# SBUF pool order, first loads and output store of a bandwidth-bound decode kernel

## The chip, the cores and the metric

One core of one Trainium2 chip runs the whole kernel. The metric is the device time of one execution in microseconds (us), as the median of several executions. The profile's span (first to last instruction) is about 1.8 us shorter than that time. A kernel's executions agree to about 0.15% either way, so differences of a few tenths of a per cent need several rounds.

Three sources are used. The *profile* is one traced execution, with its page and its views (chain of waits, windows, timeline). The *packet records* of the same trace hold start, duration and size of each DMA packet (one contiguous piece that one of the 16 DMA engines moves), but not which engine it was. The *built program* holds each tile's address in SBUF, the on-chip memory of 128 partitions into which the loads go. In the views PE is TensorE, PEld its weight loads, DVE VectorE, ACT ScalarE and POOL GpSimd; SyncE (SP) only issues loads and stores and waits.

## The reference

A decode step: `xn = layernorm(x)`, then `x + attention(xn) + mlp(xn)`, for 4 batch rows of width 576.

```python
# attention: 32 query heads, 16 K/V heads, a window of the last 2048 of 8192 positions, head size 128
q = (xn @ wq) ;  k, v = k_cache[:, :, Sk - W:], v_cache[:, :, Sk - W:]
o = softmax(q k^T * 128**-0.5) v ;  attn = o @ wo
# mlp (w1 and w2 drop out: with one position every shifted group is zero)
h2 = gelu(layernorm(xn) @ w3) @ w4
out = x + attn + xn + h2
```

The kernel must read 64 MB of K and V (1024 x 1024 bytes to the MB here; 16 heads, 2 MB each of K and V) and 19 MB of weights: 87.17 million bytes in all. It computes very little per byte.

## The kernel before

Everything is loaded in one sequence on the SyncE queue: x, wq, then K and V head by head, w3 after the third V, wo in four parts, w4 at the end. Seven K/V buffers let the loads run ahead. Pools are laid out in SBUF in the order in which they are opened.

```python
const = ctx.enter_context(tc.tile_pool(name="const", bufs=1))      # small tiles of many sizes
small = ctx.enter_context(tc.tile_pool(name="small", bufs=2))
kvp   = ctx.enter_context(tc.tile_pool(name="kv", bufs=NKV))       # NKV = 7, 16 KB per partition each
ktp, ptp = ...                                                     # work tiles (cut)
wp    = ctx.enter_context(tc.tile_pool(name="w", bufs=1))          # wq, later w3, later w4
wop   = ctx.enter_context(tc.tile_pool(name="wo", bufs=2))
...
x_bf = const.tile([B, D], BF16)
nc.sync.dma_start(out=x_bf[:], in_=x2)
wq_main = A_wq[0:KJ * P, :].rearrange("(p j) n -> p j n", j=KJ)
for j in range(KJ):                                                # 4 loads, 8 KB per partition
    nc.sync.dma_start(out=wq_sb[:, j * NQ:(j + 1) * NQ], in_=wq_main[:, j, :])
...
def load_kv(kind, h):                                              # one DMA, 128 packets of 16 KB
    t = kvp.tile([P, NC, Dh], BF16, tag="kv", name=f"{kind.lower()}n")
    nc.sync.dma_start(out=t[:].rearrange("p c d -> p (c d)"),
                      in_=win[:, h].rearrange("b (p c) d -> p b (c d)", c=NC))
...
W4_PIECES = [0, NFH // 2, NFH, NFH + 9, NFH + 14, NF]              # w4 in five loads, the last small
...
def acc_matmuls(lhsT, rhs):          # output: 4 column groups, batch rows at partitions 0,32,64,96 + b
    for i in range(NQD):
        nc.tensor.matmul(out=acc[i * QD:i * QD + B, :], lhsT=lhsT, rhs=rhs[:, i * CW:(i + 1) * CW], ...)
...
nc.vector.tensor_copy(out=fin[:], in_=acc[:])
for i in range(NQD):                                               # four output stores, two queues
    eng = nc.sync if i % 2 == 0 else nc.scalar
    eng.dma_start(out=o2[:, i * CW:(i + 1) * CW], in_=fin[i * QD:i * QD + B, :])
```

## Time and profile before

| | before |
|---|---|
| time, median | 216.3 us (216.18 to 216.32, 3 runs) |
| HBM read | 87.17 MB, 428 GB/s in the middle of the run |
| first wq packet starts | 2.15 us |
| last w4 load lands | 210.21 us |
| start of the final cast to the end of the span | 3.61 us |

These are lines of the page of the kernel before: the span, each engine's busy share, then for 40 equal slices the busy share of the DMA engines in tenths and the rate, and at the end the queue that fetches instructions (packets, MB, share).

```profile
span 214.6 us, 6449 instructions
## 1 busy us (share of the span) xinstructions
PE 121.0 (56%) x2893; PEld 94.9 (44%) x2893; DVE 118.0 (55%) x223; ACT 70.1 (33%) x258; POOL 6.1 (3%) x14
...
DMA  5999999999999999999999999999999999999960
GB/s 207 429 437 434 428 429 425 425 425 437 426 429 423 437 431 419 439 425 434 431 428 425 428 428 430 422 434 431 429 418 428 437 419 425 437 427 422 419 262 12
DMA packets 7123, 87.58 MB, mean 408 GB/s; under 512 B 820, under 2 KB 824, under 8 KB 1336
...
q8 instruction: 22, 0.36, 0.6%
...
```

No compute engine is near full, and the DMA row is at 9 from the second slice to the third last. This kernel is as long as its load stream plus the two ends of it. The windows view of the same kernel shows how much of each stretch the DMA engines used; the last two columns are their busy share and the rate in GB/s.

```profile
core 0: us, PE busy (x) PEld busy (x) DVE busy (x) ACT busy (x) POOL busy (x), PEclk, DMA share, GB/s
0.00:2.00 2.00, 0.00 (x0) 0.00 (x0) 0.64 (x2) 0.00 (x0) 1.31 (x10) 1.00 0.01 2
2.00:14.00 12.00, 3.99 (x122) 3.76 (x123) 5.78 (x10) 0.00 (x0) 4.29 (x3) 1.00 1.00 403
14.00:200.00 186.00, 109.72 (x2551) 85.51 (x2548) 109.87 (x205) 68.29 (x252) 0.54 (x1) 1.00 1.01 428
200.00:205.00 5.00, 4.12 (x123) 3.36 (x124) 1.35 (x5) 1.83 (x7) 0.00 (x0) 1.00 1.00 417
205.00:208.00 3.00, 1.71 (x81) 1.36 (x74) 0.09 (x1) 0.00 (x0) 0.00 (x0) 1.00 0.59 244
208.00:212.00 4.00, 1.42 (x36) 0.89 (x35) 0.31 (x1) 0.00 (x0) 0.00 (x0) 0.59 0.15 58
...
```

The stream holds 428 GB/s for 186 us. It has not begun in the first two microseconds, and from 205 us on it dies away: some DMA engines have finished and others have not. The end of the chain of waits (start, length, what) says what the end waits for: the last load, the last 16 matmuls, the cast.

```profile
...
182.78 27.43 DMA w_sb<-in_B_w_dram
210.21 0.04 issue
210.26 0.68 PE acc L247 x16
210.93 0.02 issue
210.96 0.31 DVE fin L480
```

On the SyncE timeline the first issue is x, so wq's first issue starts only at 1.16 us; the last line holds two of the four stores. The other two stand on the ACT timeline, shown after it.

```profile
0.73 0.36 SPq L87 DMA_DIRECT2D x_bf<-in_A_x_dram  x1
1.16 2.06 SPq L92 DMA_DIRECT2D wq_sb<-in_A_wq_dram  x4
3.26 0.44 SPq L93 DMA_DIRECT2D wq_sb<-in_A_wq_dram  x1
...
211.29 0.63 SPq L483 DMA_DIRECT2D out_dram<-fin  x2
```

```profile
211.30 0.92 ACTq L483 DMA_DIRECT2D out_dram<-fin  x2
```

### The profile page before, as it was taken

The page shows a single profiled execution, that of the slowest core. Times are in us where ns is not written, and L with a number is a line of the kernel's source. Part 1 is how long each engine was busy: PE and PEld are TensorE (multiplying, and loading weights), DVE is VectorE, ACT ScalarE, POOL GpSimd, SP SyncE. Part 2 cuts the span into 40 slices and gives each one's busy share as a digit, 9 for nine tenths or more (in the row PEclk, how much of TensorE's full clock was granted, in tenths as well). Part 3 has the DMA queues.
Part 4 walks back from the last instruction along what each step waited for, and adds up shares of the span by engine and source line. Part 5 has one row for each costly group of instructions (what it writes and reads, how often), then busy time and mean ns, then how long its engine had stood idle before and what let it go on. Part 6 is the DMA issues. An engine that isn't in the chain of part 4 may idle for free. (4 is left out here: it accounts for less than half of the span.)

```text
span 214.6 us, 6449 instructions
## 1 busy us (share of the span) xinstructions
PE 121.0 (56%) x2893; PEld 94.9 (44%) x2893; DVE 118.0 (55%) x223; ACT 70.1 (33%) x258; POOL 6.1 (3%) x14
## 2 busy tenths in 40 slices
PE   0461355647470017157999577677474705779752
PEld 0350143445360015145899456555453604557641
DVE  5608799766470047348610798785573924854210
ACT  0000005571634001607070045570725340709600
POOL 5400100000000000000000000000000000000000
PEclk9999999999999999999999999999999999999995
DMA  5999999999999999999999999999999999999960
GB/s 207 429 437 434 428 429 425 425 425 437 426 429 423 437 431 419 439 425 434 431 428 425 428 428 430 422 434 431 429 418 428 437 419 425 437 427 422 419 262 12
DMA packets 7123, 87.58 MB, mean 408 GB/s; under 512 B 820, under 2 KB 824, under 8 KB 1336
## 3 DMA queue, kind: packets, MB, share of 16 engines
q1 hardware_dynamic: 7080, 87.17, 95.7%
q8 instruction: 22, 0.36, 0.6%
q14 instruction: 5, 0.04, 0.0%
q10 hardware_dynamic: 16, 0.00, 0.0%
HBM read 87.17 MB, written 0.00 MB: 406 GB/s over the span
## 5 line engine op out<-in xcount | busy, mean ns | idle before, releaser
L302 ACT ACTIVATE pt<-S 32x128 bf16<-32x128 f32 x256 | 68.5, 268 | 92.0 <-issue 55.3
L259 DVE STREAM_TRANSPOSE kt<-kn 128x1024 int32<-128x1024 int32 x64 | 74.3, 1205 | 11.4 <-DMA kn<-in_A_k_cache_dram 11.4
L313 PE MATMUL O<-pt,vn 128*128 128x8 bf16 x1024 | 37.4, 169 | 43.2 <-DMA vn<-in_A_v_cache_dram 41.7
L313 PEld LDWEIGHTS <-vn 128*128 128x128 bf16 x1024 | 34.4, 105 | 51.3 <-DMA vn<-in_A_v_cache_dram 43.6
L273 PE MATMUL S<-qz,kt 128*128 128x32 bf16 x1024 | 39.1, 189 | 25.2 <-DVE kt L259 25.2
L273 PEld LDWEIGHTS <-kt 128*128 128x128 bf16 x1024 | 33.6, 106 | 36.1 <-DVE kt L259 30.4
L287 DVE TENSOR_REDUCE m<-mxT 8x1 f32<-8x128 f32 x16 | 4.4, 277 | 42.6 <-PE mxT L285 42.6
L316 PE MATMUL O<-pt,ones_bf 128*128 128x64 bf16 x128 | 17.1, 226 | 0.0
L302 ACT ACT_TABLE_LOAD x1 | 1.3, 1283 | 32.6 <-DVE mx L280 32.6
L368 PEld LDWEIGHTS <-w_sb 128*128 128x128 bf16 x144 | 11.4, 164 | 0.5 <-issue 0.4
L368 PE MATMUL AB<-ln2T,w_sb 128*128 128x4 bf16 x144 | 11.5, 202 | 0.0
L280 DVE TENSOR_REDUCE mx<-S 128x8 f32<-128x512 f32 x16 | 10.4, 652 | 1.0 <-PE S L273 1.0
L295 PE MATMUL S<-dg,ones_bf 8*128 8x512 bf16 x16 | 9.6, 601 | 0.1
L265 PE MATMUL S<-negbig,ohT 4*128 4x512 bf16 x16 | 9.6, 601 | 0.0
L316 PEld LDWEIGHTS <-ones_bf 128*128 128x128 bf16 x128 | 8.4, 104 | 0.0
L370 PE MATMUL AB<-ln2T,w_sb 128*128 128x4 bf16 x36 | 7.3, 202 | 0.0
L247 PE MATMUL acc<-w_sb,gT 128*4 128x144 bf16 x144 | 4.8, 294 | 2.8 <-DMA w_sb<-in_B_w_dram 2.8
L324 DVE TENSOR_REDUCE dn<-O 128x8 f32<-128x64 f32 x16 | 3.3, 208 | 5.5 <-PE O L316 5.5
L375 DVE COPY g_x<-AB 128x144 f32<-128x144 f32 x1 | 0.3, 307 | 10.7 <-PE AB L370 10.7
L285 PE MATMUL mxT<-ident_f,mx 128*8 128x128 f32 x16 | 6.0, 374 | 0.3 <-DVE mx L280 0.3
L370 PEld LDWEIGHTS <-w_sb 128*128 128x128 bf16 x36 | 5.9, 165 | 0.0
L247 PEld LDWEIGHTS <-gT 128*4 128x4 bf16 x144 | 3.4, 104 | 3.6 <-issue 3.5
(72 smaller groups left out, 64.9 us busy)
## 6 DMA issues: line engine op xcount, KB each, us to landing
kn<-in_A_k_cache_dram SPq DMA_DIRECT2D x16, 2048.0 KB, 29.3
vn<-in_A_v_cache_dram SPq DMA_DIRECT2D x16, 2048.0 KB, 27.0
wo_sb<-in_A_wo_dram SPq DMA_DIRECT2D x4, 1152.0 KB, 28.8
w_sb<-in_B_w_dram SPq DMA_DIRECT2D x2, 2304.0 KB, 31.8
wq_sb<-in_A_wq_dram SPq DMA_DIRECT2D x4, 1024.0 KB, 4.9
w_sb<-in_B_w_dram SPq DMA_DIRECT2D x3, 1296.0 KB, 32.8
w_sb<-in_B_w_dram SPq DMA_DIRECT2D x2, 576.0 KB, 32.2
w_sb<-in_B_w_dram SPq DMA_DIRECT2D x1, 720.0 KB
```

Of the source, the lines that this page charges most:

```text
L247: nc.tensor.matmul(out=acc[i * QD:i * QD + B, :], lhsT=lhsT, rhs=rhs[:, i * CW:(i + 1) * CW], start=False, stop=False, skip_group_check=True)
L259: nc.vector.transpose(out=kt[:], in_=src)
L265: nc.tensor.matmul(out=S_ps[h][:].rearrange("p g k j -> p (g k) j"), lhsT=ohT[:], rhs=nb, start=True, stop=False, skip_group_check=True)
L273: nc.tensor.matmul(out=S_ps[h][:, s * (SC // NQD) + g].rearrange("p k j -> p (k j)"), lhsT=kt[:, ib, g * NQD:(g + 1) * NQD, e:2 * QD:2].re ...
L280: nc.vector.reduce_max(out=mx[:], in_=S_ps[h][:].rearrange("p g k j -> p j (g k)"), axis=AX.X)
L285: nc.tensor.transpose(out=mxT[:], in_=st[h][:], identity=ident_f[:])
L295: nc.tensor.matmul(out=S_ps[h][:].rearrange("p g k j -> p (g k) j"), lhsT=ones_bf[0:NJ, :], rhs=dg, start=False, stop=False, skip_group_ch ...
L302: nc.scalar.activation(out=PT[h][kb * QD:(kb + 1) * QD, :, c4, :], in_=S_ps[h][c4 * QD:(c4 + 1) * QD, :, kb, :], func=ACT.Exp, scale=scale)
L313: nc.tensor.matmul(out=O_ps[h][:, 0:NJ], lhsT=vn[:, g * NQD + s, :], rhs=pt[:, g, s, :], start=(g == 0 and s == 0), stop=False, skip_group ...
L316: nc.tensor.matmul(out=O_ps[h][:, NJ:].rearrange("p (c j) -> p c j", j=NJ), lhsT=ones_bf[:], rhs=pt[:, g:g + DG, s, :], start=False, stop= ...
L368: nc.tensor.matmul(out=g_ps[:, i, :], lhsT=w3[:, j * F + e * (F // 2) + f0:j * F + (e + 1) * (F // 2):NFH], rhs=ln2T[:, j, :], start=False ...
L370: nc.tensor.matmul(out=g_ps[:, i, :], lhsT=w3[:, KJ * F + f0:KJ * F + F // 2:NFH], rhs=ln2T[:, KJ + e, :], start=False, stop=False, skip_g ...
```

## The change

Its intent, as far as the code tells it: start the weight stream earlier and with larger packets, keep the big tiles' addresses independent of the small ones, and end with one store instead of four. For the one store the batch rows must stand at equal distances, so each group of 32 partitions holds its 4 rows 8 apart, and the left operand of the accumulation gets 32 columns, of which 28 are zero.

```diff
+    kvp = ctx.enter_context(tc.tile_pool(name="kv", bufs=NKV))
+    wp = ctx.enter_context(tc.tile_pool(name="w", bufs=1))
+    wop = ctx.enter_context(tc.tile_pool(name="wo", bufs=2))
+    ktp, ptp ...
     const = ctx.enter_context(tc.tile_pool(name="const", bufs=1))
     small = ctx.enter_context(tc.tile_pool(name="small", bufs=2))
-    kvp, ktp, ptp, wp, wop ...
...
-    nc.sync.dma_start(out=x_bf[:], in_=x2)
+    nc.scalar.dma_start(out=x_bf[:], in_=x2)
-    for j in range(KJ):
-        nc.sync.dma_start(out=wq_sb[:, j * NQ:(j + 1) * NQ], in_=wq_main[:, j, :])
+    wq_main = A_wq[0:KJ * P, :].rearrange("(p j) n -> p (j n)", j=KJ)
+    for e in range(2):
+        lo, hi = e * 2 * NQ, (e + 1) * 2 * NQ
+        nc.sync.dma_start(out=wq_sb[:, lo:hi], in_=wq_main[:, lo:hi])
...
+    RS = QD // B                                       # 8
+    idz = const.tile([B, QD], F32)                     # the identity with its columns 8 apart
-    gT = const.tile([P, NF, B], BF16)
+    gT = const.tile([P, NF, QD], BF16)                 # op likewise; both zeroed once
...
-            nc.tensor.matmul(out=acc[i * QD:i * QD + B, :], lhsT=lhsT, ...
+            nc.tensor.matmul(out=acc[i * QD:(i + 1) * QD, :], lhsT=lhsT, ...
...
-    for i in range(NQD):
-        eng = nc.sync if i % 2 == 0 else nc.scalar
-        eng.dma_start(out=o2[:, i * CW:(i + 1) * CW], in_=fin[i * QD:i * QD + B, :])
+    nc.sync.dma_start(out=o2.rearrange("b (i n) -> i b n", i=NQD), in_=fin[0:P:RS, :])
```

One consequence is in no line of the diff. The first K/V buffer starts at byte 38,144 of each partition before and at byte 16,512 after. The first is 149 x 256; the second is 64 x 256 + 128. Every K, V, wq, w3, w4 and wo tile moves in the same way from a multiple of 256 to 128 past one.

More of the change, by code (lines that the diff above doesn't have):

```diff
@@ L71 @@
     ctx.enter_context(tc.manual_schedule())
+    kvp = ctx.enter_context(tc.tile_pool(name="kv", bufs=NKV))
+    wp = ctx.enter_context(tc.tile_pool(name="w", bufs=1))
+    wop = ctx.enter_context(tc.tile_pool(name="wo", bufs=2))
+    ktp = ctx.enter_context(tc.tile_pool(name="kt", bufs=3))
+    ptp = ctx.enter_context(tc.tile_pool(name="pt", bufs=3))
     const = ctx.enter_context(tc.tile_pool(name="const", bufs=1))
     small = ctx.enter_context(tc.tile_pool(name="small", bufs=2))
-    kvp = ctx.enter_context(tc.tile_pool(name="kv", bufs=NKV))
-    ktp = ctx.enter_context(tc.tile_pool(name="kt", bufs=3))
-    ptp = ctx.enter_context(tc.tile_pool(name="pt", bufs=3))
-    wp = ctx.enter_context(tc.tile_pool(name="w", bufs=1))
-    wop = ctx.enter_context(tc.tile_pool(name="wo", bufs=2))
     ps_s = ctx.enter_context(tc.tile_pool(name="ps_s", bufs=3, space=PSUM))
@@ L83 @@
     ps_acc = ctx.enter_context(tc.tile_pool(name="ps_acc", bufs=1, space=PSUM))
-    x_bf = const.tile([B, D], BF16)
-    nc.sync.dma_start(out=x_bf[:], in_=x2)
-    wq_main = A_wq[0:KJ * P, :].rearrange("(p j) n -> p j n", j=KJ)
-    wq_sb = wp.tile([P, KJ * NQ + NQ // 2], BF16, tag="w", name="wq_sb")
-    for j in range(KJ):
-        nc.sync.dma_start(out=wq_sb[:, j * NQ:(j + 1) * NQ], in_=wq_main[:, j, :])
-    nc.sync.dma_start(out=wq_sb[:, KJ * NQ:], in_=A_wq[KJ * P:D, :].rearrange("r (e f) -> (r e) f", e=2))
     w_tiles = {}
@@ L109, in load_kv @@
         kv_tiles[kind, h] = t
+    x_bf = const.tile([B, D], BF16)
+    nc.scalar.dma_start(out=x_bf[:], in_=x2)
+    wq_sb = wp.tile([P, KJ * NQ + NQ // 2], BF16, tag="w", name="wq_sb")
+    wq_main = A_wq[0:KJ * P, :].rearrange("(p j) n -> p (j n)", j=KJ)
+    for e in range(2):
+        lo, hi = e * 2 * NQ, (e + 1) * 2 * NQ
+        nc.sync.dma_start(out=wq_sb[:, lo:hi], in_=wq_main[:, lo:hi])
+    nc.sync.dma_start(out=wq_sb[:, KJ * NQ:], in_=A_wq[KJ * P:D, :].rearrange("r (e f) -> (r e) f", e=2))
     def load_wo(p):
@@ L184, with k_transpose @@
     xnT = transposed(xn_bf, "xnT")
+    kts = {}
+    def k_transpose(h, s):
+        src = kv_tiles["K", h][:].bitcast(I32)[:, s * SC:(s + 1) * SC, :].rearrange("p c (ib i) -> p ib c i", i=QD)
+        kt = ktp.tile([P, 2, SC, QD], I32, tag="kt")
+        nc.vector.transpose(out=kt[:], in_=src)
+        kts[h, s] = kt
     for j in range(KJ):
@@ L232 @@
     nc.vector.reduce_sum(out=own[:], in_=ident_f[:].rearrange("p (h d) -> p h d", h=WOH), axis=AX.X)
-    xsum = const.tile([B, D], F32)
+    idz = const.tile([B, QD], F32)
+    nc.gpsimd.memset(idz[:], 0.0)
+    nc.gpsimd.tensor_copy(out=idz[:, 0:QD:RS], in_=ident_f[0:B, 0:B])
+    xsum = xn_f
     nc.vector.tensor_tensor(out=xsum[:], in0=xn_f[:], in1=x_bf[:], op=ALU.add)
     for i in range(NQD):
-        nc.tensor.matmul(out=acc[i * QD:i * QD + B, :], lhsT=ident_f[0:B, 0:B], rhs=xsum[:, i * CW:(i + 1) * CW],
+        nc.tensor.matmul(out=acc[i * QD:(i + 1) * QD, :], lhsT=idz[:], rhs=xsum[:, i * CW:(i + 1) * CW],
                          start=False, stop=False, skip_group_check=True)
@@ L241 @@
     ln2T = transposed(ln2_bf, "ln2T")
-    gT = const.tile([P, NF, B], BF16)
+    gT = const.tile([P, NF, QD], BF16)
+    nc.gpsimd.memset(gT[:], 0.0)
+    op = const.tile([P, WOR, QD], BF16)
+    nc.gpsimd.memset(op[:], 0.0)
     def acc_matmuls(lhsT, rhs):
         for i in range(NQD):
-            nc.tensor.matmul(out=acc[i * QD:i * QD + B, :], lhsT=lhsT, rhs=rhs[:, i * CW:(i + 1) * CW],
+            nc.tensor.matmul(out=acc[i * QD:(i + 1) * QD, :], lhsT=lhsT, rhs=rhs[:, i * CW:(i + 1) * CW],
                              start=False, stop=False, skip_group_check=True)
-    kts = {}
     S_ps = {}
@@ L254 @@
     st = {}
-    def k_transpose(h, s):
-        src = kv_tiles["K", h][:].bitcast(I32)[:, s * SC:(s + 1) * SC, :].rearrange("p c (ib i) -> p ib c i", i=QD)
-        kt = ktp.tile([P, 2, SC, QD], I32, tag="kt")
-        nc.vector.transpose(out=kt[:], in_=src)
-        kts[h, s] = kt
     def k_mask(h):
@@ L350, in o_pick @@
                                 in1=own[:].unsqueeze(1).unsqueeze(3).to_broadcast([P, WOR, WOH, B]), op=ALU.mult)
-        op = small.tile([P, WOR, B], BF16, tag="op")
         with nc.allow_low_precision("one term is not zero"):
-            nc.vector.reduce_sum(out=op[:], in_=mk[:].rearrange("p i h b -> p i b h"), axis=AX.X)
-        st["op"] = op
+            nc.vector.reduce_sum(out=op[:, :, 0:QD:RS], in_=mk[:].rearrange("p i h b -> p i b h"), axis=AX.X)
     def o_proj(h):
@@ L358, in o_proj @@
             return
-        op = st.pop("op")
         for i in range(WOR):
@@ L381, in mlp_act @@
         nc.vector.tensor_scalar(out=u[:], in0=u[:], scalar1=0.5, scalar2=0.5, op0=ALU.mult, op1=ALU.add)
-        nc.vector.tensor_tensor(out=gT[:], in0=u[:], in1=xs[:], op=ALU.mult)
+        nc.vector.tensor_tensor(out=gT[:, :, 0:QD:RS], in0=u[:], in1=xs[:], op=ALU.mult)
     def mlp_out(lo, hi):
```

## The prediction

> **What bounds the kernel.** It streams HBM. The page shows 87.17 MB, a DMA share of 9 tenths or more in 37 of 40 slices, 420 to 437 GB/s; PE is 56% busy, DVE 55%. The chain of waits ends with the last w4 load (to 210.2 us), 0.68 us of matmuls, a 0.31 us cast, the stores and the closing barrier; the span is 214.6 us. The windows show three stretches where the stream is not full:
> - Start: the first wq bytes move at 2.15 us; the ramp costs about another 0.6 us (164, then 360 GB/s).
> - Tail: from 205 us the DMA share falls to 0.68, 0.55, 0.41, 0.18. In the packet records a third of the 16 DMA engines finish at about 209.8 us, 4 to 5 us after the first. They lag in steps of 1 to 1.4 us; I blame the 22 instruction fetches of 16 KB (about 0.93 us each).
> - End: fin is ready at 211.27 us; four stores leave from two queues, the last issued on ACT at 211.95 us; its landing is seen at about 213.7 us.
>
> **What the change does, costed.**
> 1. x leaves SyncE's queue: its issue starts at 0.73 us, the first wq issue at 1.16 us (timeline), so the stream starts 0.43 us earlier. The Trainium skill, "DMA: Bandwidth & Descriptors", "Issuing engines are not separate DMA queues", says that another queue saves issue time only. x may land 1 us later behind cold wq packets, but the K transposes start only at 26 us and the load queue is filled past 45 us: no cost.
> 2. wq in 16 KB packets: packets follow each other every 607 ns at 16 KB and 174 ns at 4.6 KB, so about 4.6 ns per packet beyond its bytes; 16 fewer per DMA engine save 0.07 us. The ramp may gain another 0.1 us.
> 3. One store: by the waits at the end, the last landing moves from 213.7 to about 213.2 us: 0.5 us.
> 4. acc matmuls with 32 columns for 4: same count, same 144 columns moved; LDWEIGHTS take 104 ns with 4 columns, 105 with 128. No change. Strided gT and op writes and four GpSimd operations are off the path.
> 5. Pool order: the built program puts K, V, weights at addresses 128 past a multiple of 256 bytes; they were on multiples. The same page, "How a descriptor splits into AXI transactions", says that a start off 256 bytes costs extra beats. Here w4's second piece starts so (source and destination), and its 10,368 B packets take the same 389 ns as those of the two on the grid. I expect nothing; at 4 beats of 516 (an estimate from that page) it would be 0.8%, 1.6 us.
>
> The tail stays: as many PE instructions, hence fetches.
>
> **Sum.** -0.43 - 0.07 - 0.1 - 0.5 = -1.1 us: 215.2 us, range 214.1 to 216.8. Chances: faster by over 2% 0.03, within 2% 0.94, slower by over 2% 0.03.
>
> **What would show it.** Timeline: the first SyncE issue is wq at 0.73 us, data from about 1.7 us. Windows: 428 GB/s in the middle; the last w4 landing 0.6 us before 210.2. K and V packets still 611 ns. Cast's end to span's end 2.8 us, not 3.3.
>
> **What would make it wrong.** An effect of the new SBUF addresses; another spread of the fetches over the DMA engines, which would move the tail either way.

## The result and the profile after

| | before | after |
|---|---|---|
| time, median of 6 runs each | 216.31 us (216.18 to 216.54) | 217.06 us (216.68 to 217.15) |
| span of the profiled run | 214.57 us | 214.90 us |
| first wq packet starts | 2.15 us | 1.74 us |
| last w4 load lands | 210.21 us | 211.19 us |
| cast start to span end | 3.61 us | 3.19 us |
| 16 KB packet of K or V, mean, after 30 us | 611.0 ns | 614.2 ns |
| instruction fetch of 16 KB, mean of 22 | 935 ns | 1068 ns |

Here and below, packet means of K and V leave out the few packets that took over 0.65 us (18 of 3,712 before, 19 after). Of the 19 K and V packets over 0.8 us in the kernel before, 17 overlap an instruction fetch.

The ratio is 1.003 (95% interval 1.0017 to 1.0043): 0.3% slower, where 0.5% faster was predicted.

The page after, in the lines that answer to those of before:

```profile
span 214.9 us, 6449 instructions
...
DMA  6999999999999999999999999999999999999960
GB/s 245 436 433 424 427 427 419 430 424 424 438 415 417 433 436 416 432 424 421 427 430 421 427 424 427 424 427 421 422 433 419 419 436 427 424 423 414 424 283 27
...
q8 instruction: 22, 0.36, 0.7%
...
```

The first slice moved more (245 in place of 207 GB/s) and the middle moved less. The windows say how much less:

```profile
core 0: us, PE busy (x) PEld busy (x) DVE busy (x) ACT busy (x) POOL busy (x), PEclk, DMA share, GB/s
0.00:2.00 2.00, 0.00 (x0) 0.00 (x0) 0.64 (x2) 0.00 (x0) 1.31 (x10) 1.00 0.42 92
2.00:14.00 12.00, 3.42 (x107) 3.27 (x108) 5.78 (x10) 0.00 (x0) 4.85 (x5) 1.00 0.96 401
14.00:200.00 186.00, 109.32 (x2553) 85.53 (x2551) 110.94 (x205) 67.58 (x248) 1.96 (x3) 1.00 1.01 425
200.00:205.00 5.00, 3.67 (x105) 3.03 (x102) 0.66 (x4) 2.77 (x11) 0.00 (x0) 1.00 1.01 422
205.00:208.00 3.00, 2.34 (x75) 2.05 (x72) 0.85 (x2) 0.00 (x0) 0.00 (x0) 1.00 0.72 300
208.00:212.00 4.00, 2.01 (x72) 1.52 (x71) 0.29 (x1) 0.00 (x0) 0.00 (x0) 1.00 0.26 106
...
```

In the long middle stretch the rate is 425 in place of 428 GB/s. That looks like nothing, but 0.7% of 186 us is 1.3 us, more than all the predicted gains together. The chain of waits after shows the last load later, at 211.19 us:

```profile
...
183.93 27.26 DMA w_sb<-in_B_w_dram
211.19 0.04 issue
211.23 0.46 PE acc L263 x16
211.69 0.02 issue
211.71 0.31 DVE fin L486
```

The timelines confirm what the diff intended: SyncE's first issue is wq, x is issued at the same moment on the ScalarE queue, and one store ends the kernel. Its issue takes 0.70 us, a little more than two of the old ones together (0.63). First SyncE after, then ACT after:

```profile
0.73 0.86 SPq L109 DMA_DIRECT2D wq_sb<-in_A_wq_dram  x2
1.64 0.43 SPq L110 DMA_DIRECT2D wq_sb<-in_A_wq_dram  x1
...
212.04 0.70 SPq L487 DMA_DIRECT2D out_dram<-fin  x1
```

```profile
0.73 0.56 ACTq L104 DMA_DIRECT2D x_bf<-in_A_x_dram  x1
```

x is not late either: the first layernorm instruction starts at 2.20 us, and at 2.18 us before.

### The profile page after: what moved, and what is told of

It is laid out like the page before. It is cut to its first block, busy times and chain, and to the rows that moved or that the text cites. A ratio compares the mean times of both kernels' runs of the same rounds, so it can differ in the third digit from the quotient of the medians.

```text
span 214.9 us, 6449 instructions
## 1 busy us (share of the span) xinstructions
PE 120.8 (56%) x2893; PEld 95.4 (44%) x2893; DVE 119.2 (55%) x223; ACT 70.3 (33%) x258; POOL 8.1 (4%) x18
## 3 DMA queue, kind: packets, MB, share of 16 engines
q1 hardware_dynamic: 6788, 87.17, 96.0%
HBM read 87.17 MB, written 0.00 MB: 406 GB/s over the span
## 5 line engine op out<-in xcount | busy, mean ns | idle before, releaser
L263 PE MATMUL acc<-w_sb,gT 128*32 128x144 bf16 x144 | 4.5, 291 | 2.3 <-DMA w_sb<-in_B_w_dram 2.3
L199 PE MATMUL AB<-xnT,wq_sb 128*128 128x4 bf16 x128 | 3.7, 166 | 2.3 <-DMA wq_sb<-in_A_wq_dram 2.0
```

The costliest lines, as they stand in the source:

```text
L263: nc.tensor.matmul(out=acc[i * QD:(i + 1) * QD, :], lhsT=lhsT, rhs=rhs[:, i * CW:(i + 1) * CW], start=False, stop=False, skip_group_check= ...
```

## The experiments

The first question was the middle of the run. Three theories were put up. A: what counts is the SBUF destination's place on a grid of 256 bytes. R: the new start brings the 16 DMA engines into a worse spacing. R2: low SBUF addresses are slower. The first job ran four kernels on one chip (before there: 216.21 us). All kernels of this section passed the comparison with the reference, even the four that are wrong: presumably attention adds too little to the output for its tolerance.

### Put the tiles back on the grid (e1)

```diff
# in the changed kernel
+    padp = ctx.enter_context(tc.tile_pool(name="pad", bufs=1))
+    padp.tile([P, 64], BF16, name="pad")                # 128 bytes, nothing else
     kvp = ctx.enter_context(tc.tile_pool(name="kv", bufs=NKV))
```

> The changed kernel with a 128-byte pad ahead of the K/V pool, so K, V and all weight tiles start on a multiple of 256 bytes again (pool order kept). Theory A (an SBUF destination 128 off the 256-byte grid slows the packets): 16 KB packets back to 611 ns and 215.3 us, range 215.0 to 215.6, that is 0.8% under the changed kernel. Rival R (the new start, 16 KB wq packets and x on another queue, brings the DMA engines into a worse spacing): packets up to 619 ns and about 217.0 us. Rival R2 (the low addresses of K and V are slower): also about 217.0 us.

Measured: 215.48 us, ratio to before 0.9968 (0.9955 to 0.998). K and V packets are back at a mean of 611.0 ns and the fetches at 930 ns. In its windows the middle is back at 428 GB/s:

```profile
...
0.00:2.00 2.00, 0.00 (x0) 0.00 (x0) 0.64 (x2) 0.00 (x0) 1.32 (x10) 1.00 0.50 101
...
14.00:200.00 186.00, 110.10 (x2572) 86.22 (x2570) 111.00 (x205) 68.72 (x252) 1.96 (x3) 1.00 1.01 428
...
205.00:208.00 3.00, 1.47 (x78) 1.13 (x69) 0.00 (x0) 0.00 (x0) 0.00 (x0) 1.00 0.54 222
...
```

The end of its chain:

```profile
...
209.73 0.04 issue
209.77 0.70 PE acc L265 x13
210.47 0.02 issue
210.49 0.31 DVE fin L488
```

An unused tile of 128 bytes turns 0.3% slower into 0.3% faster. Theory A's forecast comes true, those of R and R2 do not: pool order, start and end are all unchanged here. The gain over before, 0.73 us, is less than the 1.1 us of the prediction without the offset; more of that below.

### Take the kernel before off the grid (e2)

```diff
# in the kernel before: the same pad ahead of kvp, so K and V start at 38,272 = 149 x 256 + 128
```

> The kernel before with the same 128-byte pad ahead of its K/V pool, so its K, V and weight tiles start 128 past a multiple of 256; nothing else. Theory A: 16 KB packets spread from 611 to about 619 ns as in the changed kernel, and about 217.7 us (217.2 to 218.2). R and R2: 216.3 us and 611 ns.

Measured: 217.84 us, ratio 1.0077 (1.0064 to 1.009), packets 614.2 ns on average, 48% of them over 613 ns, up to 626. The middle is at 425 GB/s again:

```profile
...
14.00:200.00 186.00, 108.78 (x2520) 84.70 (x2517) 109.50 (x203) 67.19 (x247) 0.55 (x1) 1.00 1.01 425
...
```

The cost of the offset alone is 1.6 us, in a kernel that has nothing else of the change.

### The two pool orders (e3, e4)

```diff
# e3: the changed kernel with the old pool order (K, V, weights at 224 past a multiple of 256)
# e4: the kernel before with the new pool order (128 past)
```

> The changed kernel with the pool order of before: K, V and weights lie behind the larger constants, at 224 past a multiple of 256. Theory A: packets slower than 611 ns, time as the changed kernel (217.0 us) or longer, since 224 is off the grid too. R: 217.0 us. R2: about 215.3 us with packets of 611 ns.

> The kernel before with the new pool order alone: K and V low in SBUF, at 128 past a multiple of 256. Theory A: as the padded kernel before, about 217.7 us with packets up to 619 ns. R: 216.3 us. R2: about 217.7 us. Against the padded kernel before it tells A from R2: equal under A, slower under R2.

Measured: e3 217.63 us (1.0067), mean packet 615.6 ns; e4 217.78 us (1.0074), 614.3 ns. e4 equals the padded kernel before (217.84), so the region of SBUF shows no effect. e3 suggests why the pool order is in the change at all: gT and op grew, and in the old order their sizes would have pushed K and V to 224 past the grid, slower still than 128 past (217.63 against 217.06 us). The new order fixed the address, at one that is off the grid too.

### Which grid, and how far off it (e7, e11)

```diff
# e7: the pad is 384 bytes (tiles on a multiple of 512); e11: 192 bytes (64 past a multiple of 256)
```

> The changed kernel with a pad of 384 bytes: K, V and weights start on a multiple of 512 bytes (the 128-byte pad put them 256 past one). If 256 bytes is the grid that counts: equal to the 128-byte pad, about 215.4 us, 0.3% under before. If a coarser grid helps more: below 215.0 us. If the 128-byte pad's gain was luck of one address: back near 217.

> The changed kernel with a pad of 192 bytes: K, V and weights start 64 past a multiple of 256. At 128 past, the changed kernel took 217.0 us; at 224 past, 217.6. If only being off the 256-byte grid counts: 217.0. If the cost grows as the first and last pieces get smaller or less even: 217.2 to 217.6. If 64 bytes is grid enough: 215.5.

Measured on one chip (before there: 216.34 us): e7 215.46 us (0.9955, 0.9942 to 0.9969), 611.0 ns; e11 217.20 us (1.0039, 1.0026 to 1.0052), 614.7 ns. A coarser grid than 256 gains nothing that can be told from the 128-byte pad, and a multiple of 64 is not enough.

### Destination, source, or their difference (e8, e9)

My prediction had dismissed the offset because w4's second piece starts 128 past the grid and its packets took the same 389 ns as its neighbours. In that piece source and destination are both off by 128. So theory M: only a difference between the two costs.

```diff
# e8 = the padded kernel before, e9 = the kernel before, each with this (the result is wrong on purpose):
-    in_=win[:, h].rearrange("b (p c) d -> p b (c d)", c=NC)
+    in_=win[:, h, (Sk - W) * Dh - Dh // 2:Sk * Dh - Dh // 2].rearrange("b (p n) -> p b n", p=PB)
     # win is the cache with positions and head size flattened: 64 elements, 128 bytes earlier
```

> The padded kernel before (K and V tiles 128 past a multiple of 256) with the K and V sources also moved back by 128 bytes, so source and destination stand equally off the grid; the result is wrong on purpose. Theory M (what costs is source and destination standing differently on the grid; that is why w4's second piece, off the grid on both sides, showed nothing): K and V packets 611 ns, time near 216.5 us, the weights alone still paying. Theory A (the destination alone counts): packets 611 to 619 ns as in the padded kernel, about 217.8 us.

> The kernel before (tiles on the grid) with the K and V sources moved back by 128 bytes; the result is wrong on purpose. Theory M: packets spread to 619 ns and about 217.5 us. Theory A: 611 ns and 216.3 us. A third reading, that the source off the grid costs extra beats by itself: all packets evenly longer, about 615.7 ns[...], about 217.7 us.

Measured on one chip (before there: 216.10 us): e8, both off, 218.52 us (1.0108, 1.0092 to 1.0123); e9, source alone, 217.52 us (1.0063, 1.0049 to 1.0077). Theory M fell at once: both off is the slowest of all. Theory A seemed to fall too, since e9 lost 1.4 us where it expected none. The packet records separate the two costs. The times at which the stream had started its 10th to 80th million bytes, in us:

```
                              10 M     15 M     20 M     40 M     80 M   | K, V packets after 36 us, mean
before                       26.11    37.79    49.54    96.26   190.16   | 611.0 ns
e2  destination off          25.93    37.81    49.53    96.58   191.25   | 614.2 ns
e9  source off               26.15    38.65    50.21    97.06   190.92   | 611.0 ns
e8  both off                 26.20    38.57    50.18    97.25   191.89   | 613.9 ns
```

With the destination off, the delay grows to the end, because the packets are longer all the way. With the source off, 0.7 to 0.9 us are lost once, before the 15th million, where single packets take up to 0.8 us; after it the packets and the pace are those of the kernel before. With both off, both are lost. So the destination's place is what costs all through the run (theory A), and the source has another cost, early and once, whose cause I did not settle. In e9's packet records four of the five last engines end 0.5 to 0.8 us later than the last group before (at 210.2 to 210.3 us), and one alone at 211.2 us. That this one ends 1.4 us later, and not 0.8, is not explained either.

The Trainium skill, "DMA: Bandwidth & Descriptors", section "How a descriptor splits into AXI transactions", says that a descriptor that does not start on a multiple of 256 bytes begins its first transaction at the boundary below, and that the unused bytes still cost beats. For 128 off the grid that is an estimated 4 extra beats of 32 bytes, and at the 27.2 GB/s of one engine (the slope of duration against size in these records) 4.7 ns per packet. No run here shows such evenly longer packets: with the source off they take 611 ns as ever, and with the destination off they take anything from 611 to 626. (The addresses in HBM are not in the built program; that the tensors start on the grid is assumed.)

### The two predicted gains, one at a time (e5, e6, e15, e13)

```diff
# e5: the kernel before + x on the ScalarE queue + wq in two pieces of 16 KB packets
# e6: the kernel before + 32-column accumulation + one store, padded so that K, V, weights stay on the grid
```

> The kernel before with only the new start: x on the ScalarE queue, wq in two pieces of 16 KB packets; K, V and weights stay on the 256-byte grid. The prediction's terms: -0.43 us (earlier first byte) -0.07 -0.1, so about 215.6 us, 0.6 us under before. From the padded runs, where start and store together gave 0.73 us, I now expect less: 0.3 to 0.5 us under before.

> The kernel before with only the new end: batch rows 8 partitions apart, 32-column accumulation, one output store; a pad keeps K, V and weights on the 256-byte grid. The prediction's term: -0.5 us, about 215.7 us. From the padded runs: 0.3 to 0.5 us under before; cast end to span end 2.9 us in place of 3.3.

Measured on one chip (before there: 216.10 us): e5 216.04 us (0.9995, 0.9982 to 1.0007); e6 216.31 us (1.0006, 0.9994 to 1.0019). Each alone shows nothing, against 0.3 to 0.5 us expected, yet together, in the padded kernel, they gave 0.73 us. The traces say where a part of it goes. In e5 the last load lands at 209.86 us, 0.35 us earlier, but the closing part grows from 3.61 to 3.67 us. (The trace of the kernel before is of another job, in which that kernel took 216.31 us for 216.10 here. So about 0.2 of the 0.35 us may be the job's, and where the rest of the 0.41 us of the earlier start went in e5 is not shown.) In e6 the closing part is 3.66 us, no shorter than with four stores.

SyncE's recorded instructions in the closing part (us after the start of the cast; the first column is the number of the instruction in SyncE's record, counted from 0) tell why:

```
e6, 85 recorded               e1 (padded), 82 recorded         e13, 77 recorded (below)
1.06  wait 1.07 for store     1.23  wait 0.89 for store        ...
2.18  wait                    2.15  wait                       2.12  wait
2.25  wait                    2.24  wait                       2.19  wait
2.32  wait                    2.32  drain                      2.25  wait
2.79  wait     no. 79         2.37  drain                      2.31  drain
2.88  drain                   2.85  barrier  no. 79            2.38  drain
2.97  drain                   2.95  drain                      2.53  barrier
3.12  barrier                 3.11  barrier                    2.62  drain
3.21  drain                                                    3.00  barrier
3.60  barrier
```

In all 16 traces that have an instruction no. 79, SyncE pauses about 0.45 us before it, whatever it is. In the kernel before and in e6 that is one of the waits that hold up the closing barrier. With the new start *and* the single store SyncE has four instructions fewer than before, so the pause slips into the barrier, where GpSimd goes on meanwhile. This was put to the test from both sides.

```diff
# e15: the padded changed kernel + three tiny unused loads on SyncE in mid-run
+        for i in range(3):
+            nc.sync.dma_start(out=x_again[i][:], in_=x2[:, 0:16])
# e13: the padded changed kernel with fewer SyncE instructions:
#      wq main part 2 -> 1 load, w3 main part 2 -> 1, w4 5 -> 4, first wo load on the ScalarE queue
```

> The changed kernel with the 128-byte pad and three extra tiny loads on SyncE in mid-run (32 bytes for each of 4 rows, not used). In all traces SyncE pauses about 0.45 us before its 79th recorded instruction. Theory P (the pause stands at a fixed place of SyncE's instruction stream; the new start and the single store pay for the end only because together they move that place into the closing barrier): 85 instructions instead of 82, so the pause falls among the closing waits again as with the store alone: cast start to span end about 3.65 us in place of 3.17, and about 215.9 us. Rival (the end is shorter because of the single store itself, or the two parts interact in another way): cast start to span end stays 3.2 us and 215.5 us.

> A candidate, and the other side of that test: the changed kernel with the 128-byte pad and about four SyncE instructions fewer (wq and w3 in one piece each for their main parts, w4's first two pieces as one, the first wo load on the ScalarE queue). Theory P: with fewer than 79 recorded instructions there is no pause; cast start to span end 2.9 to 3.2 us, and 215.1 to 215.5 us. Rival: no change at the end, 215.5 us.

Measured on one chip (before there: 216.10 us): e15 215.88 us (0.9991, 0.9979 to 1.0004), closing part 3.67 us, pause before no. 79 among the waits. e13 215.34 us (0.9964, 0.9951 to 0.9976), closing part 3.07 us, no pause. Three loads of 128 bytes each undo the whole gain of the end. The place of the pause is shown; what SyncE does in it is not. No packet of an instruction queue is recorded in it (in the kernel before: 213.2 to 213.7 us). It follows the count of *recorded* instructions although their mix differs (52 DMA issues among the first 79 before, 48 in e1), so the recording itself may make it; no run rules that out.

### The tail (e10, e14)

From 205 us on, some DMA engines still work and others are idle. The prediction blamed the 22 instruction fetches of 16 KB. Two kernels take fetches away by leaving out matmuls; their results are wrong.

```diff
# e10, e14: the kernel before with fewer probabilities-times-V matmuls
-        for g in range(CG):
+        for g in range(0, CG, 2)        # e10;  range(0, CG, 8) in e14
# e14 also: one of the four score matmuls per group
-            for ie in range(4):
+            for ie in range(1):
```

> The kernel before with every second matmul of probabilities times V left out (512 of 2893 matmuls and their weight loads; the result is wrong on purpose). TensorE is not on the chain until the last loads land. Theory F (the 4 to 5 us tail is made by instruction fetches that run on a few DMA engines): 22 fetches become about 18, the last w4 landing comes about 0.8 us earlier and the time falls to about 215.5 us (215.0 to 215.8). Rival (the lag of those engines has another cause): 216.2 us.

> The kernel before with seven of eight probabilities-times-V matmuls and three of four score matmuls left out (the result is wrong on purpose): 2452 TensorE instructions in place of 5781, so about 9 instruction fetches for 22. Theory F (each fetch delays the one DMA engine that carries it, and the engine with the most fetches ends last): the last w4 landing comes at about 207 to 208 us in place of 210.2, and 213.5 to 214.5 us. Rival (the lag has another cause): no earlier than 209.8 us, and 216 us.

Measured: e10 216.24 us (0.9993, 0.9979 to 1.0007; before there 216.34), with 18 fetches; the last load lands only 0.16 us earlier. That alone spoke against the theory. In its packet records, though, the last group is 3 engines (209.1 to 209.7 us) instead of 5 (209.4 to 209.8): taking away four fetches had thinned the last group without emptying it. e14 goes further: 214.68 us (0.9929, 0.9914 to 0.9944; before there 216.10). Span and instruction fetches of e14, then the end of its chain:

```profile
span 213.0 us, 3120 instructions
...
q8 instruction: 9, 0.15, 0.2%
...
```

```profile
...
208.60 0.04 issue
208.64 0.68 PE acc L247 x13
209.32 0.02 issue
209.35 0.31 DVE fin L480
```

With 9 fetches the last load lands at 208.60 us, 1.6 us earlier (some 0.2 of it between the jobs), on the unchanged 87.17 MB. In its records, chained as described in the next section, 6 engines finish by 205.4 us, as in the kernel before, nine at 206.5 to 207.0 us, and one at 208.2 us; the last fetch began at 204.9 us. That is the picture of one delay of 1.2 to 1.4 us for each fetch on the engine that carries it, and the slowest engine ends the kernel. The time was 0.2 us and the landing 0.6 us above the ranges that I gave for the theory, and the fetches' engines are not in the records, so the assignment is inferred; that leaving out TensorE instructions brings the last load forward is shown. It did not do so by faster packets: K and V took 611.0 ns as before, and the first six engines end within 0.2 us of where they did. The Trainium skill, "Runtime: NRT & Kernel Launch", section "Instruction fetch mechanics", says that instructions are refilled in blocks of 16 KiB, 256 of them, and that crossing into the next block is mostly hidden. 5786 TensorE instructions (2893 matmuls, each with its weight load) and 22 fetches, 2458 and 9, agree with the block size. That the crossings are not hidden from the DMA stream is what e14 points to; whether TensorE waits at them no run here shows.

### A candidate with fewer instructions (e12)

```diff
# e12: the padded changed kernel; denominators summed in 64 matmuls of 128 columns for 128 of 64
-    DG = 8
+    DG = 16
```

> A candidate: the 128-byte pad on the changed kernel, and the denominators summed by one matmul of 128 columns per slice in place of two of 64 (64 matmuls and 64 weight loads fewer, 8 KB of instructions). Theory F: half a fetch less, so 0 to 0.3 us under the padded kernel, about 215.3 us; otherwise the same as it, 215.5 us.

Measured: 215.32 us (0.9957, 0.9944 to 0.9969; before there 216.34); 22 fetches as before. It can't be told from the 512-byte pad of the same job (0.9955). e1, e7, e12 and e13 all beat both kernels, by 0.3 to 0.5% against the kernel before, and none of them stands out.

## Why the prediction was wrong

**The step that failed is point 5, "I expect nothing" of the new addresses.** It cost 1.6 us (217.84 against 216.21 us in the padded kernel before). The sum had this term at zero. The same point named 1.6 us as what it would be if the expectation failed, its estimate from 4 beats of 516, and named it again as the first thing that could make the prediction wrong; the range up to 216.8 did not hold it. The agreement in size is partly luck, because the cost is made up differently. In the worst engine's work it is, from the records of before and after: 32 K and V tiles x 8 packets x 3.2 ns = 0.8 us; the weights' packets, some 2 to 4 ns each, about 0.25 us; and 3 instruction fetches that take 0.13 us longer each, 0.4 us (three, if the 4.3 us between the first and the last group of engines, worked out below, are 3 steps of 1.4). Together about 1.5 us. From the landings: the last one came 0.98 us later although the first packet came 0.41 us earlier, so 1.39 us were lost between.

The prediction's second risk, another spread of the fetches, can be looked for by chaining each packet to the one that starts where it ends (an inference, since the records hold no engine). Before, six engines end first (205.2 to 205.4 us), then two, three and, last, five (209.4 to 209.8). In e2 and in the changed kernel the groups have the same sizes, so no other spread shows. In e2 the first six end 1.0 us later (206.1 to 206.7), which fits the longer packets alone, and the last five 1.35 us later (210.8 to 211.2), which fits packets and fetches.

**Why the evidence misled.** The one piece with an off-grid start, w4's second, had source and destination off together, had 128 packets where K and V have 4,096, and stood in a run in which all else was on the grid. It was taken for a control and was none. What exactly shielded it is open. It is not that both ends were off together, since e8 had that for K and V. It is not its odd size either: in the changed kernel w4's first piece, of the same size, has its destination off, and in the first 3 us of it 37% of the packets took over 390 ns, mean 391.1.

**What the cost is not.** It is no contest with the compute engines: among the changed kernel's 16 KB packets, the 369 during which VectorE, TensorE and ScalarE all stood idle took 614.3 ns on average, and all 614.0 (from 16 to 198 us). The Trainium skill, "SBUF — State Buffer", section "SBUF: two separate sides", says that engine and DMA ports can't contend; this trace agrees. What stays open is why in the changed kernel the packets off the grid took 611 ns from 7 to 18 us, while the 16 DMA engines kept one order, each starting a packet every 607 ns, and grew longer only in the time after the first instruction fetch (at 16.5 us) had set one of them back. A conflict between DMA engines that depends on their spacing would look like that, but nothing here shows it.

**Point 1, the earlier start, was right in size** (first packet 1.74 for 2.15 us, predicted 0.43), and x landed in time. The Trainium skill, "DMA: Bandwidth & Descriptors", section "Issuing engines are not separate DMA queues", says that another queue saves issue time only; the 0.41 us against x's 0.43 us on SyncE agree. **Point 2 was over-sized:** the larger wq packets were to give 0.17 us, but the first K packet, queued behind wq, starts 0.41 us earlier (13.36 for 13.77 us), no more than the start itself.

**Point 3, the one store, had the right size and the wrong reason.** The closing part fell by 0.42 us (0.5 predicted), but not because a landing came sooner: the last store's packets end 1.76 us after the cast starts, and 1.81 us before, because the one store takes 0.70 us to issue. What went is a pause of SyncE that moved. The 213.7 us that the prediction took for a landing is the wait after that pause (2.70 us after the cast starts); the stores' packets had ended at 212.8. Alone, the store gained nothing (e6).

**Point 4 was right:** the same TensorE instructions, and the last 16 matmuls 0.46 us long after and 0.68 before, which goes with the granted clock there (1.00 against 0.50 in the last microseconds), not with the columns: at 0.50 the padded kernel's 32 columns take 0.70. The weight loads of gT did grow (shortest 92 for 80 ns), at no cost that shows.

**The tail stayed** at about the same length, as said; between the means of the first and the last group of engines it went from 4.3 to 4.6 us. Without point 5 the prediction would have been close: the padded kernel took 215.48 us, 0.3 us above 215.2, of which 0.17 us is point 2.

## What to carry to other kernels

In a kernel that is bound by its loads, look up the SBUF addresses of the big tiles in the built program after every change to a small one, and keep the tiles on multiples of 256 bytes; here an unused pad of 128 bytes was worth 0.6 to 0.7%, and the rest of the change 0.3%. A piece of evidence that "shows no effect" must have the same shape as what it is to stand for: size, number, and both ends. And before adding up small gains at the end of a kernel, try them one by one and together, since a pause like SyncE's here may hide one and give back the other.

## What the Trainium skill lacked or had wrong

- "DMA: Bandwidth & Descriptors" ("How a descriptor splits into AXI transactions"): its wording is of reads, and it doesn't say what a start off the grid costs on the side that is written. An SBUF destination off the grid lengthened 16 KB packets from 611.0 to 614.2 ns on average, unevenly from 611 to 626, and the kernel by 0.8% (e2). A source off the grid left them at 611.0 ns after an early loss of 0.8 us (e9), where the estimated 4 beats more would be 4.7 ns each.
- "SBUF — State Buffer" ("Operand start alignment") states what is legal and says that its runs timed nothing. A line on speed is missing: multiples of 256 and 512 bytes were equal (215.48 and 215.46 us), 64 past cost 217.20, 128 past 217.06 and 224 past 217.63 us (kernel before in the same jobs: 216.2 to 216.3).
- "Runtime: NRT & Kernel Launch" ("Instruction fetch mechanics"): the cost of a block crossing is called mostly hidden. Each fetch took 0.88 to 0.98 us of a DMA engine in the kernel before; with 9 fetches for 22 (e14, matmuls left out) the last load landed 1.6 us earlier.
- No page has the pause of about 0.45 us that SyncE makes before its recorded instruction no. 79, in all 16 traces long enough to have one; it may be the recording's own.
- No page that I used tells what an issue costs by shape: a store of 16 rows of 288 bytes took 0.70 us to issue, one of 4 rows 0.28 to 0.29 us on SyncE.
